# Seven block products instead of eight in the down projection of the last four feed-forward units

## The chip, the cores and the metric

The kernel runs on one NeuronCore of a Trainium2 chip. The metric is the device time of one execution in microseconds. The engines that matter here are PE (matrix multiplication, with PEld as its weight loads), DVE and ACT (element-wise work, and the copies out of the matmul accumulators in PSUM), POOL (a few small instructions) and SP (which issues most DMAs). Each engine works through its own queue in order and waits at an instruction until what it needs is there.

## The reference

Two layers, each a gated long convolution over the sequence followed by a feed-forward block (SwiGLU), on 2048 rows of 512 columns; the second layer uses the same weights as the first.

```python
def _A_ref(q, k, v, shift_k, ssm_k, ssm_D):
    ...                                  # k_shift: 4-tap convolution of k along the sequence
    kv = k_shift * v
    ...                                  # y: causal convolution of kv with ssm_k over 2048 rows, by FFT
    y = y + kv * ssm_D[None, None, :]
    return q * y

def _B_ref(x, w_gate, w_up, w_down):
    g = _silu(x @ w_gate)
    u = x @ w_up
    return (g * u) @ w_down              # (2048 x 512) -> 1792 -> 512

x = A_q
x = x + _A_ref(_layernorm(x), A_k, A_v, A_shift_k, A_ssm_k, A_ssm_D)
x = x + _B_ref(_layernorm(x), B_w_gate, B_w_up, B_w_down)
x = x + _A_ref(_layernorm(x), A_k, A_v, A_shift_k, A_ssm_k, A_ssm_D)
x = x + _B_ref(_layernorm(x), B_w_gate, B_w_up, B_w_down)
```

The outputs are bf16.

## The kernel before

The sequence is cut into four blocks `c` of 512 rows, and each block into two halves `h` of 256 rows. A half is two row tiles of 128 rows. Convolution and feed-forward of the blocks are interleaved: while PE multiplies for the feed-forward of one block, DVE and ACT prepare the spectra of the next. A feed-forward *unit* is `(layer, c, h)`; there are 16, and the last four, of block 3, are (0,3,0), (0,3,1), (1,3,0) and (1,3,1). By then no convolution is left, only the rows' normalisation, the gating of the convolution's result and the feed-forward itself.

Before a unit stands its prologue (`prologue`, with `ln_stats`, `normalise`): statistics of the rows of `x` (L846, L847, L849 on DVE), their inverse standard deviation `rstd` on POOL (L851), the normalised rows `n` times the convolution's rows `Yk` (L923), added to `x` (L924), again statistics and `rstd`, normalised rows `z` (L901), and a transposing DMA from SP (L930) into `zT`. So the rows that one unit of layer 0 leaves in `x` are needed by the prologue of the unit of layer 1 with the same `c` and `h`.

A unit (`ffn`) has 14 feature tiles of 128, in groups of 4, 4, 4 and 2 (`GROUPS`). For each pair of tiles 8 matmuls of 256 columns make the gate and 8 the up projection (L348) into a PSUM bank each (`pf`, four banks). ACT applies silu to the gate into `sg` (L1005) and copies the up projection to `ht` (L1009). DVE multiplies the two for a whole group (L1012): `ht` then holds the hidden tile, transposed, bf16. The down projection (L1025) takes the hidden tile as the loaded weights and a row tile of `w_down`, 512 columns, as the moving operand: for each feature tile and each of the two row tiles one matmul, accumulated over 14 feature tiles in a bank `pd` for each row tile. ACT copies both banks to `dn` (L1065), DVE adds them to `x` (L1068), and in layer 1 SP sends the rows to the output (L1076).

The last unit (1,3,1) differs at its end: its second row tile is split into two halves of columns with a bank each, the right half gets `x` by a matmul with the identity (L980), ACT copies it out (L1039), DVE adds the left half to `x` (L1041) and the first row tile (L1032), and the two halves leave by SP and ACT (L1045).

The order on each engine isn't left to a scheduler: the program records operations with their readers and writers, and the table `ORDER` of one number for each operation, found offline by a search, gives the order in which all are issued. Buffers come from rings (`s8` with 10 large slots, `ht` with 5, the PSUM rings `pf`, `pc`, `pd` with 4, 2 and 2 banks); a slot is taken again when its last reader is done. While PE would wait at the start, `issue` puts in warm-up matmuls (`wm`, L1297).

Of the kernel before, what the change touches and what calls it, by code (L numbers as in the profile page):

```python
# [9 lines left out]
P = 128  # L10
# [17 lines left out]
GROUPS = (4, 4, 4, 2)  # L28
TINY = 0.2
# [22 lines left out]
    4, 74, 3, 1, 2, 22, 16, 12, 14, 0, 13, 15, 40, 7, 6, 5, 8, 9, 17, 11, 18, 19, 10, 20, 21, 25, 41, 42, 56, 57, 34, 35, 33, 36, 31, 32, 29, 30, 51,  # L52
    53, 52, 70, 38, 39, 45, 48, 23, 24, 26, 64, 60, 46, 44, 61, 55, 43, 66, 76, 73, 47, 37, 82, 27, 28, 62, 63, 58, 68, 54, 65, 49, 50, 59, 69, 79,
    168, 199, 216, 243, 275, 75, 93, 94, 95, 96, 80, 89, 90, 91, 92, 77, 78, 81, 84, 85, 97, 98, 99, 100, 101, 104, 103, 105, 110, 125, 134, 147, 148,
    149, 166, 178, 71, 102, 111, 116, 117, 119, 120, 121, 67, 87, 83, 88, 72, 86, 106, 107, 108, 109, 112, 113, 114, 130, 131, 132, 144, 145, 146,
    139, 140, 141, 135, 136, 137, 126, 127, 128, 118, 122, 124, 123, 115, 133, 152, 155, 161, 156, 170, 175, 138, 129, 153, 154, 142, 143, 150, 151,
    158, 160, 157, 163, 159, 164, 171, 179, 162, 165, 197, 198, 188, 211, 212, 213, 176, 167, 177, 182, 219, 227, 169, 173, 172, 174, 180, 181, 183,
    184, 189, 190, 228, 229, 208, 209, 191, 231, 210, 185, 195, 186, 192, 193, 187, 196, 194, 202, 203, 220, 224, 225, 226, 221, 222, 238, 223, 230,
    232, 242, 233, 246, 247, 268, 263, 269, 267, 270, 271, 273, 274, 272, 281, 283, 284, 304, 316, 317, 311, 312, 248, 255, 257, 256, 259, 258, 261,
    260, 214, 215, 234, 205, 206, 207, 200, 201, 204, 217, 218, 236, 325, 326, 235, 249, 321, 324, 295, 296, 308, 309, 290, 292, 299, 300, 237, 285,  # L60
    327, 329, 354, 355, 368, 367, 276, 302, 375, 613, 303, 262, 305, 319, 320, 353, 369, 373, 374, 418, 432, 413, 433, 434, 460, 459, 465, 502, 473,
    495, 494, 514, 522, 524, 556, 557, 523, 542, 536, 500, 581, 650, 626, 651, 264, 265, 244, 245, 239, 240, 250, 251, 266, 323, 322, 252, 253, 241,
    254, 278, 288, 286, 287, 289, 336, 331, 291, 294, 293, 306, 297, 298, 279, 280, 307, 337, 332, 301, 310, 313, 314, 315, 338, 333, 339, 334, 342,
    352, 366, 350, 351, 360, 361, 346, 357, 378, 422, 399, 386, 387, 402, 403, 385, 388, 364, 365, 407, 423, 430, 406, 411, 404, 405, 384, 395, 396,
    397, 412, 424, 431, 340, 341, 344, 345, 371, 437, 439, 438, 440, 441, 347, 343, 348, 356, 349, 358, 359, 370, 376, 377, 381, 382, 383, 389, 391,
    390, 393, 394, 409, 410, 419, 420, 414, 415, 451, 452, 444, 445, 453, 461, 463, 462, 464, 466, 467, 471, 470, 472, 476, 477, 501, 545, 496, 544,
    447, 450, 448, 449, 488, 489, 487, 492, 493, 509, 506, 468, 469, 491, 498, 479, 481, 456, 457, 499, 510, 534, 482, 511, 454, 486, 504, 512, 474,
    475, 517, 537, 535, 518, 519, 505, 515, 541, 584, 563, 585, 596, 624, 667, 625, 427, 421, 428, 458, 478, 484, 485, 528, 530, 532, 533, 551, 553,
    538, 540, 554, 564, 573, 574, 565, 567, 400, 503, 277, 282, 531, 560, 599, 561, 619, 620, 622, 623, 621, 648, 649, 661, 662, 723, 689, 724, 318,
    330, 335, 328, 362, 380, 392, 379, 363, 398, 372, 401, 436, 480, 483, 490, 416, 417, 408, 426, 442, 443, 425, 429, 521, 548, 598, 597, 552, 601,  # L70
    603, 618, 529, 507, 513, 516, 497, 446, 435, 520, 569, 526, 571, 508, 455, 525, 527, 539, 555, 572, 578, 617, 612, 580, 579, 652, 641, 727, 728,
    717, 718, 683, 688, 676, 677, 665, 684, 643, 644, 642, 656, 731, 732, 733, 734, 778, 765, 769, 781, 674, 543, 750, 1069, 668, 657, 670, 671, 697,
    678, 698, 699, 796, 790, 805, 806, 807, 834, 835, 846, 880, 847, 891, 895, 888, 881, 892, 894, 889, 890, 896, 910, 902, 905, 925, 900, 926, 938,
    943, 949, 996, 995, 999, 1000, 1023, 1006, 1024, 1067, 582, 583, 591, 592, 568, 586, 558, 559, 600, 610, 629, 590, 595, 549, 550, 588, 589, 593,
    594, 602, 615, 630, 604, 605, 562, 587, 608, 609, 546, 570, 614, 616, 636, 575, 576, 547, 566, 577, 627, 639, 628, 640, 653, 654, 655, 645, 659,
    606, 607, 631, 638, 646, 658, 660, 696, 702, 672, 673, 675, 681, 685, 686, 637, 647, 687, 706, 703, 611, 692, 690, 691, 664, 666, 633, 635, 693,
    707, 704, 680, 694, 679, 682, 695, 710, 705, 711, 708, 712, 760, 766, 763, 764, 744, 745, 743, 757, 767, 797, 791, 779, 780, 729, 730, 738, 739,
    771, 772, 782, 799, 801, 770, 783, 725, 726, 792, 794, 755, 756, 795, 800, 808, 788, 802, 786, 803, 804, 814, 812, 815, 813, 816, 716, 719, 714,
    720, 721, 722, 741, 740, 746, 747, 748, 751, 752, 761, 762, 768, 773, 784, 820, 785, 798, 818, 819, 817, 823, 824, 825, 842, 850, 843, 853, 855,
    862, 864, 856, 863, 865, 866, 882, 886, 908, 883, 884, 830, 831, 839, 840, 827, 828, 845, 848, 849, 877, 874, 857, 858, 832, 833, 821, 829, 838,  # L80
    844, 867, 878, 876, 861, 871, 854, 870, 869, 873, 851, 852, 887, 903, 893, 868, 872, 875, 885, 901, 904, 942, 921, 961, 963, 1053, 964, 735, 709,
    736, 737, 809, 810, 811, 911, 906, 912, 913, 914, 918, 915, 922, 923, 924, 937, 947, 948, 945, 946, 700, 701, 713, 715, 742, 753, 754, 776, 822,
    930, 931, 973, 967, 974, 984, 989, 990, 992, 1004, 1068, 1003, 1008, 634, 663, 632, 669, 774, 759, 749, 758, 859, 860, 775, 777, 933, 934, 787,
    789, 932, 952, 793, 837, 826, 836, 841, 879, 957, 958, 959, 960, 962, 981, 1074, 1018, 897, 899, 927, 907, 975, 898, 928, 991, 988, 1001, 1037,
    985, 1022, 987, 983, 1007, 1030, 1038, 1039, 1099, 1097, 1110, 1098, 1101, 1136, 1121, 1122, 1116, 1117, 1193, 1194, 1111, 1112, 1167, 1168, 1185,
    1186, 1166, 1170, 1189, 1190, 1197, 1196, 1219, 1218, 1217, 1213, 1086, 1077, 1078, 1079, 1137, 1149, 1083, 1151, 1152, 1220, 1239, 1252, 1253,
    1265, 1272, 1273, 1274, 1275, 1276, 1279, 1291, 1282, 1283, 1280, 1281, 1284, 1285, 1292, 1305, 1322, 1329, 941, 953, 916, 935, 950, 951, 909,
    920, 954, 978, 994, 968, 982, 969, 970, 976, 977, 917, 936, 986, 1011, 1009, 971, 972, 979, 980, 965, 966, 955, 956, 998, 1012, 1016, 939, 940,
    919, 929, 944, 1014, 1028, 1015, 1029, 1031, 1033, 1032, 1025, 1026, 1027, 1034, 997, 1035, 1002, 1005, 1036, 1057, 1056, 1010, 1013, 1050, 1051,
    1044, 1045, 1040, 1041, 1052, 1059, 1062, 1054, 1055, 1046, 1049, 1047, 1048, 1042, 1043, 1058, 1060, 1063, 1019, 1020, 993, 1017, 1021, 1061,  # L90
    1064, 1066, 1065, 1080, 1070, 1088, 1073, 1089, 1071, 1075, 1072, 1076, 1105, 1153, 1131, 1118, 1133, 1113, 1114, 1108, 1109, 1128, 1132, 1142,
    1154, 1155, 1139, 1141, 1134, 1135, 1100, 1115, 1093, 1119, 1145, 1156, 1159, 1147, 1148, 1091, 1092, 1150, 1157, 1160, 1158, 1161, 1162, 1081,
    1082, 1084, 1085, 1090, 1095, 1103, 1102, 1104, 1106, 1120, 1124, 1107, 1123, 1125, 1126, 1144, 1163, 1138, 1140, 1174, 1176, 1173, 1175, 1178,
    1179, 1181, 1180, 1182, 1183, 1203, 1198, 1206, 1211, 1207, 1212, 1221, 1222, 1223, 1224, 1225, 1187, 1188, 1171, 1172, 1184, 1195, 1199, 1201,
    1202, 1216, 1234, 1204, 1205, 1208, 1226, 1214, 1215, 1227, 1228, 1235, 1236, 1241, 1230, 1231, 1164, 1165, 1200, 1237, 1209, 1210, 1240, 1259,
    1242, 1229, 1243, 1191, 1192, 1244, 1266, 1245, 1286, 1264, 1302, 1512, 1342, 1094, 1087, 1129, 1146, 1130, 1169, 1238, 1246, 1249, 1247, 1250,
    1293, 1294, 1295, 1298, 1296, 1299, 1300, 1308, 1309, 1328, 1310, 1311, 1143, 1177, 1096, 1127, 1232, 1233, 1330, 1314, 1331, 1332, 1343, 1344,
# [178 lines left out]
def kernel(  # L276
# [639 lines left out]
    def prologue(layer, c, h, on_pe=False):  # L916
# [47 lines left out]
        return done, [stats]  # L964


    LAST_UNIT = (1, NB - 1, HP - 1)

    def ffn(unit):
        layer, c, h = unit  # L970
# [360 lines left out]
```

## Time and profile before

| what | value |
|---|---|
| time, median of 3 runs | 344.43 us (343.92 to 344.95) |
| profiled execution: span from first to last instruction | 342.6 us (no own time beside the span is given) |
| PE busy | 337.9 us, 99% |
| DVE busy | 283.0 us, 83% |
| ACT busy | 252.3 us, 74% |
| gate and up projections (L348, pf) | 1792 matmuls, 57.1% of the chain that ended last |
| down projection (L1025, pd) | 462 matmuls, 28.2% of the chain |

The span is the time between the core's first and last instruction; the measured time also has what lies around it. Busy time of PE counts matmuls that overlap each other, so it says that PE had work, not how fast it went; the pace is read from long stretches of one kind in the chain. A chain is followed back from the last instruction, at each step to what released it. In a group of instructions the columns are: line, engine, operation, output and inputs, shapes, count, then busy time in us and the mean of one in ns, then the engine's idle time just before them and what ended it.

### The profile page before, as it was taken

How to read it: one execution, taken by the hardware profiler on the slowest of the kernel's cores; microseconds unless marked ns; L12 is line 12 of the kernel's file. 1: busy time of each engine (PE TensorE's matmuls, PEld its weight loads, DVE VectorE, ACT ScalarE, POOL GpSimd, SP SyncE). 2: the span in 40 equal slices, each digit the busy share in tenths (PEclk: the TensorE clock that was granted, in tenths of full speed). 3: DMA queues.
4: the chain of work that ended last, by engine and by line, in shares of the span. 5: the costliest groups of instructions: out<-in, count | busy, mean ns of one | idle time of the engine just before them, and what ended most of it. 6: DMA issues, size and time to landing. Idle time of an engine off the chain costs nothing.

```text
span 342.6 us, 6609 instructions
## 1 busy us (share of the span) xinstructions
PE 337.9 (99%) x2622; PEld 248.3 (72%) x2622; DVE 283.0 (83%) x482; ACT 252.3 (74%) x504; POOL 39.7 (12%) x46
## 2 busy tenths in 40 slices
PE   8999999999999999999999999999999999999996
PEld 7647867768686767768587767768675877777783
DVE  7999999999999999999999999989996524635122
ACT  6899999999984768868999955959474655446351
POOL 3000110103010101221010100100601000000000
PEclk9999999999999999999999999999999999999999
DMA  7999015130116056010101047000102010101001
GB/s 281 323 311 337 5 30 96 31 94 0 34 31 124 33 122 124 3 29 2 33 17 34 15 141 106 12 20 1 34 0 47 16 49 0 42 6 25 10 15 46
DMA packets 42088, 22.95 MB, mean 67 GB/s; under 512 B 33861, under 2 KB 39882, under 8 KB 42058
## 3 DMA queue, kind: packets, MB, share of 16 engines
q1 hardware_dynamic: 41904, 22.47, 26.2%
q8 instruction: 20, 0.33, 0.4%
q14 instruction: 10, 0.08, 0.1%
q10 hardware_dynamic: 154, 0.07, 0.1%
HBM read 12.33 MB, written 2.10 MB: 42 GB/s over the span
## 4 chain that ended last, share of the span: by engine, by line
PE 98%; ACT 1%; DVE 0%; issue 0%
PE pf L348 57%; PE pd L1025 28%; PE ps L348 8%; PE ps L495 2%; PE ps L834 1%; PE wm L1297 1%; ACT hs L524 1%; ACT X L456 0%; PE pt L403 0%; PE ptz L957 0%; PE pt L514 0%; DVE hs L530 0%; ACT xc L1039 0%; ACT nmr L889 0%; PE pt L1162 0%
## 5 line engine op out<-in xcount | busy, mean ns | idle before, releaser
L348 PE MATMUL pf<-zT,wg_sb 128*128 128x256 bf16 x896 | 110.2, 273 | 0.0
L348 PE MATMUL pf<-zT,wu_sb 128*128 128x256 bf16 x896 | 109.9, 273 | 0.0
L1025 PE MATMUL pd<-wd_sb,ht 128*128 128x512 bf16 (+1 forms) x462 | 103.9, 373 | 0.0
L348 PEld LDWEIGHTS <-wg_sb 128*128 128x128 bf16 x896 | 87.7, 98 | 16.0
L348 PEld LDWEIGHTS <-wu_sb 128*128 128x128 bf16 x896 | 87.7, 98 | 15.9
L1005 ACT ACTIVATE sg<-pf 128x512 bf16<-128x512 f32 x112 | 66.5, 607 | 23.8 <-PE pf L348 19.1
L1025 PEld LDWEIGHTS <-ht 128*128 128x128 bf16 x462 | 45.1, 98 | 44.6 <-DVE ht L1012 1.2
L1009 ACT CAST ht<-pf 128x512 bf16<-128x512 f32 x112 | 64.5, 593 | 14.5 <-PE pf L348 14.2
L1012 DVE TENSOR_TENSOR ht<-ht,sg 128x1024 bf16<-128x1024 bf16 (+1 forms) x64 | 38.9, 618 | 23.0 <-ACT ht L1009 13.3
L851 POOL TENSOR_TENSOR rstd<-ve,nhalf 128x2 f32<-128x2 f32 x24 | 27.7, 1155 | 210.3 <-DVE ve L849 210.3
L1065 ACT CAST dn<-pd 128x512 bf16<-128x512 f32 x30 | 17.1, 591 | 33.8 <-PE pd L1025 23.7
L846 DVE BATCH_NORM_STATS2 bnst<-xc 128x6 f32<-128x512 bf16 x48 | 31.6, 684 | 0.7
L690 DVE TENSOR_TENSOR t<-X,G 128x2048 bf16<-128x2048 bf16 x18 | 22.0, 1220 | 0.1
L694 DVE TENSOR_TENSOR t<-X,G 128x2048 bf16<-128x2048 bf16 x18 | 21.9, 1217 | 0.0
L1068 DVE TENSOR_TENSOR xc<-xc,dn 128x1024 bf16<-128x1024 bf16 x15 | 10.2, 682 | 12.1 <-ACT dn L1065 12.1
L456 ACT ACTIVATE X<-ps 128x512 bf16<-128x512 f32 x32 | 19.2, 608 | 0.7 <-PE ps L495 0.5
L877 POOL TENSOR_TENSOR rstd<-ve,nhalf 128x2 f32<-128x2 f32 x8 | 8.6, 1080 | 60.1 <-ACT ve L875 60.1
L923 DVE TENSOR_TENSOR n<-n,Yk 128x1024 bf16<-128x1024 bf16 x15 | 10.4, 690 | 6.1 <-ACT Yk L728 5.2
L704 DVE TENSOR_TENSOR Z<-Z,t 128x2048 bf16<-128x2048 bf16 x12 | 14.7, 1223 | 0.3
L702 DVE TENSOR_TENSOR t<-t,t 128x2048 bf16<-128x2048 bf16 x12 | 14.7, 1223 | 0.3
L456 ACT ACTIVATE H<-ps 128x512 bf16<-128x512 f32 x24 | 13.9, 619 | 0.0
L348 PE MATMUL ps<-hs,fwd 128*128 128x512 bf16 x40 | 12.8, 379 | 0.5 <-ACT hs L524 0.3
(105 smaller groups left out, 323.4 us busy)
## 6 DMA issues: line engine op xcount, KB each, us to landing
hn<-in_A_ssm_k_dram SPq DMA_DIRECT2D x4, 512.0 KB, 5.9
vt<-in_A_v_dram SPq DMA_DIRECT2D x4, 512.0 KB, 6.1
xc<-in_A_q_dram SPq DMA_DIRECT2D x4, 512.0 KB, 6.9
out_dram<-xc SPq DMA_DIRECT2D x15, 128.0 KB, 1.8
wg_sb<-in_B_w_gate_dram SPq DMA_DIRECT2D x1, 1792.0 KB
wu_sb<-in_B_w_up_dram SPq DMA_DIRECT2D x1, 1792.0 KB, 8.2
wd_sb<-in_B_w_down_dram SPq DMA_DIRECT2D x1, 1280.0 KB, 13.1
kn<-in_A_k_dram SPq DMA_DIRECT2D x1, 512.0 KB, 4.7
```

Source lines behind the costliest of these rows:

```text
L348: nc.tensor.matmul(o, lhsT=lhsT, rhs=rhs, start=(n == 0), stop=(n == len(terms) - 1))
L456: add("ACT", act(D), lambda: nc.scalar.activation(out=view(), in_=ps.t[:], func=ACT.Copy, scale=scale), r=[ps], w=[(buf, keys)], conv=conv)
L690: dve(n * D, lambda t1=t1, part=part: nc.vector.tensor_mul(out=t1.t[:], in0=x.t[:, sl, 0, :], in1=g.t[:, sl, part, :]), [(x, key(slots, (0 ...
L694: dve(n * D, lambda t2=t2, part=part: nc.vector.tensor_mul(out=t2.t[:], in0=x.t[:, sl, 1, :], in1=g.t[:, sl, 1 - part, :]), [(x, key(slots ...
L702: dve(n * D, lambda t1=t1, t2=t2, comb=comb: nc.vector.tensor_tensor(out=t1.t[:], in0=t1.t[:], in1=t2.t[:], op=comb), [t2], [t1], conv=conv)
L846: add("DVE", 0.6, lambda st=st, i=i: nc.vector.bn_stats(out=st.t[:], in_=xs[c].t[:, i, :]), r=[(xs[c], (i,))], w=[st])
L851: add("POOL", pw, lambda: nc.gpsimd.tensor_tensor(out=rstd.t[:], in0=ve.t[:], in1=nhalf.t[:].to_broadcast((P, n)), op=ALU.pow), r=[ve, nha ...
L1005: add("ACT", act(D), lambda ps=ps, o=o, sg=sg: nc.scalar.activation(out=sg.t[:, o:o + 2, :], in_=ps.t[:], func=ACT.Silu), r=[ps], w=[(sg, ...
L1009: add("ACT", act(D), lambda ps=ps, o=o, ht=ht: nc.scalar.copy(out=ht.t[:, o:o + 2, :], in_=ps.t[:]), r=[ps], w=[(ht, (o // 2,))], due=(uni ...
L1012: dve(n * W, lambda sg=sg, ht=ht: nc.vector.tensor_mul(out=ht.t[:], in0=ht.t[:], in1=sg.t[:]), [sg], [ht], due=(unit, k / pairs, 0.0, "h"))
L1025: nc.tensor.matmul((pds[o] if not cs.start else pds[HP]).t[:, cs], lhsT=ht.t[:, q, o * P:(o + 1) * P], rhs=wt["d"].t[:, ft, cs], start=(ft ...
L1065: add("ACT", act(D), lambda o=o: nc.scalar.copy(out=dn.t[:, o, :], in_=pds[o].t[:]), r=[pds[o]], w=[(dn, (o,))], due=(unit, 1.0, 3.0, "h"))
```

## The change

For block 3 the down projection of a pair of feature tiles and the two row tiles, a product of 2 x 2 blocks (row tile x feature tile times feature tile x half of the columns), is computed by Strassen's scheme in its seven-product form: seven matmuls of 256 columns where there were four of 512 (eight blocks). `STRASSEN` says for how many groups of each unit: all four for (0,3,0), (0,3,1) and (1,3,0), the first two for (1,3,1). 25 pairs of feature tiles are meant.

`weight_sums` makes, once, sums and differences of blocks of `w_down` for all pairs, in three slots of `s8`. `seven` makes for each group five sums and differences of hidden tiles (`cb`) on DVE and issues the products into four PSUM banks `ps7` (two of `pd`, two of `pc`), two products side by side in three of them. `add_seven` copies the four banks to SBUF on ACT (`mt`) and adds them into `x` with five DVE instructions; it takes the place of the copies to `dn` and the one addition. In the last unit the products come first, the last two groups go as before, and the identity matmul (`first_half`) stands behind `add_seven`, as it reads the `x` that this leaves. The table `ORDER` is a new one for the whole program.

```diff
+STRASSEN = {(0, 3, 0): 4, (0, 3, 1): 4, (1, 3, 0): 4, (1, 3, 1): 2}
...
 ORDER = [
...
+    C = D // 2
+    ws = {}
+
+    def weight_sums():
...
+        ev = lambda sl: wd.t[:, 0::2, sl]
+        od = lambda sl: wd.t[:, 1::2, sl]
+        lo, hi = slice(0, C), slice(C, D)
+        a = ws["14"] = new("s8", "wsa", [P, 2, NF // 2, C], parts=2)
+        b = ws["3"] = new("s8", "wsb", [P, NF // 2, C])
+        c = ws["67"] = new("s8", "wsc", [P, NF, C])
+        for out, keys, x0, x1, op in (
+                (lambda: a.t[:, 0], [(a, (0,))], lambda: ev(lo), lambda: od(hi), ALU.add),
+                (lambda: b.t[:], [b], lambda: ev(hi), lambda: od(hi), ALU.subtract),
+                (lambda: a.t[:, 1], [(a, (1,))], lambda: od(lo), lambda: ev(lo), ALU.subtract)):
+            dve(NF // 2 * C, lambda out=out, x0=x0, x1=x1, op=op: nc.vector.tensor_tensor(out=out(), in0=x0(), in1=x1(), op=op),
+                [wd], keys)
...
+    def seven(unit, banks, ht, fts, first, last):
+
+        m = len(fts) // 2
+        f0 = fts[0] // 2
+        cb = new("s8", "cb", [P, 5, m, P], parts=3)
+        e, q, r, o = banks
...
+        dve(2 * m * P, lambda: nc.vector.tensor_add(
+            out=strided(cb.t[:], 0, [[P, m], [m * P, 2], [1, P]]), in0=strided(ht.t[:], 0, [[2 * W, m], [P, 2], [1, P]]),
+            in1=strided(ht.t[:], W, [[2 * W, m], [P, 2], [1, P]])), [ht], [(cb, (0,))], **kw)
...
+        for bank, rd, terms in (
+                (e, [ht, ws["14"], ws["3"]], (
+                    (0, lambda i: ht.t[:, 2 * i + 1, P:2 * P], lambda i: ws["14"].t[:, 1, f0 + i]),
+                    (1, lambda i: ht.t[:, 2 * i, 0:P], lambda i: ws["3"].t[:, f0 + i]))),
+                (q, [(cb, (0,)), wd], (
+                    (0, lambda i: cb.t[:, 0, i], lambda i: wd.t[:, 2 * (f0 + i) + 1, C:D]),
+                    (1, lambda i: cb.t[:, 1, i], lambda i: wd.t[:, 2 * (f0 + i), 0:C]))),
+                (r, [(cb, (1,)), ws["67"]], (
+                    (0, lambda i: cb.t[:, 3, i], lambda i: ws["67"].t[:, 2 * (f0 + i) + 1]),
+                    (1, lambda i: cb.t[:, 2, i], lambda i: ws["67"].t[:, 2 * (f0 + i)]))),
+                (o, [(cb, (2,)), ws["14"]], (
+                    (0, lambda i: cb.t[:, 4, i], lambda i: ws["14"].t[:, 0, f0 + i]),))):
+            def go(bank=bank, terms=terms):
+                for half_, lhsT, rhs in terms:
+                    for i in range(m):
+                        nc.tensor.matmul(bank.t[:, half_ * C:(half_ + 1) * C], lhsT=lhsT(i), rhs=rhs(i),
...
+    def add_seven(unit, banks):
...
+        for n, bank in enumerate(banks):
+            k = C if n == 3 else D
+            add("ACT", act(k), lambda n=n, bank=bank, k=k: nc.scalar.copy(out=mt.t[:, n, 0:k], in_=bank.t[:, 0:k]), r=[bank], w=[(mt, (n,))],
...
+        dve(2 * D, lambda: nc.vector.tensor_add(out=x.t[:, span(rows), :], in0=x.t[:, span(rows), :],
+                                                in1=mt.t[:, 0:1, :].to_broadcast((P, 2, D))), [(mt, (0,))], [(x, rows)], **kw)
+        dve(D, lambda: nc.vector.tensor_add(out=strided(x.t[:], at + C, [[1, D]]), in0=strided(x.t[:], at + C, [[1, D]]), in1=mt.t[:, 1]),
+            [(mt, (1,))], [(x, rows)], **kw)
+        dve(D, lambda: nc.vector.tensor_sub(out=two(2), in0=two(2), in1=two(1)), [(mt, (1,))], [(mt, (2,))], **kw)
+        dve(D, lambda: nc.vector.tensor_add(out=two(2), in0=two(2), in1=mt.t[:, 3:4, 0:C].to_broadcast((P, 2, C))), [(mt, (3,))],
+            [(mt, (2,))], **kw)
+        dve(D, lambda: nc.vector.tensor_add(out=ends(), in0=ends(), in1=two(2)), [(mt, (2,))], [(x, rows)], **kw)
...
             dve(n * W, lambda sg=sg, ht=ht: nc.vector.tensor_mul(out=ht.t[:], in0=ht.t[:], in1=sg.t[:]), [sg], [ht],
                 due=(unit, k / pairs, 0.0, "h"))
+            if gi < sevens:
+                seven(unit, banks, ht, fts, gi == 0, gi == sevens - 1)
+                if gi == sevens - 1:
+                    add_seven(unit, banks)
+                    if unit == LAST_UNIT:
+                        first_half()
+                continue
...
     for c in range(NB):
+        if (0, c, 0) == min(STRASSEN):
+            weight_sums()
         run((0, c, 0))
```

## The prediction

> **What bounds the kernel now.** I read the page's busy times and slices first, then the chain of waits in order of time, then the windows of the last stage, then the groups by form and the timeline of POOL. All durations below are from that one profiled execution. Its span is 342.6 us; no time of its own is given beside the span, so I put the sum against the median of the runs, 344.43, and carry the 1.8 us that lie around the span unchanged (the three runs lie between 343.92 and 344.95).
>
> ```profile
> PE 337.9 (99%) x2622; PEld 248.3 (72%) x2622; DVE 283.0 (83%) x482; ACT 252.3 (74%) x504; POOL 39.7 (12%) x46
> ...
> DVE  7999999999999999999999999989996524635122
> ACT  6899999999984768868999955959474655446351
> ...
> PEclk9999999999999999999999999999999999999999
> ```
>
> PE is busy throughout, at full granted clock. DVE is full for about three quarters of the span and half idle in the last quarter. The chain says where PE's time counts one to one:
>
> ```profile
> 22.47 0.91 ACT hs L524
> 23.38 0.04 issue
> ...
> 33.37 7.87 PE pf L348 x72
> ...
> 285.14 11.35 PE pf L348 x104
> 296.50 6.04 PE pd L1025 x28
> 302.54 6.99 PE pf L348 x64
> ...
> 333.15 6.09 PE pd L1025 x42
> 339.24 0.02 issue
> 339.26 0.37 ACT xc L1039
> ```
>
> From 33.37 to 339.24 the chain is PE alone. It gives PE's pace: 11.35/104 = 109.1 ns for a matmul of 256 columns, 6.04/28 = 215.7 ns for one of 512. The last stretch agrees: 14 of 512 and 28 of 256 columns (also with ht loaded as weights) make 6.08, shown 6.09. Only before 33 us does PE wait for others, and after 339.24 come one copy and the last output DMA.
>
> ```profile
> 200.00:225.00 25.00, 25.00 (x181) 17.42 (x179) 24.66 (x40) 14.86 (x32) 1.75 (x2) 1.00 0.47 95
> ...
> 280.00:290.00 10.00, 10.00 (x70) 6.74 (x69) 3.23 (x9) 4.09 (x8) 0.69 (x1) 1.00 0.00 0
> 290.00:300.00 10.00, 10.00 (x77) 7.35 (x75) 6.37 (x14) 4.87 (x9) 0.69 (x1) 1.00 0.17 41
> ```
>
> The columns are PE, PEld, DVE, ACT, POOL. Until 250 us DVE has no room (24.66 of 25); between 260 and 330 the seven windows of 10 us leave DVE 41.6 us and ACT 35.4 us idle. The four units of block 3, which the change touches, run there.
>
> ```profile
> L1012 DVE TENSOR_TENSOR ht<-ht,sg 128x1024 bf16<-128x1024 bf16 x48 | 32.8, 685 | 19.3 <-ACT ht L1009 13.3 <-ACT sg L1005 6.0
> ...
> L1065 ACT CAST dn<-pd 128x512 bf16<-128x512 f32 x30 | 17.1, 591 | 33.8 <-PE pd L1025 23.7 <-DVE xc L1068 6.0 <-issue 4.1
> ...
> L561 DVE TENSOR_TENSOR vt<-ps,vt 128x512 bf16<-128x512 f32 x4 | 2.7, 692 | 0.4 <-PE ps L348 0.4
> ...
> L1012 DVE TENSOR_TENSOR ht<-ht,sg 128x512 bf16<-128x512 bf16 x16 | 6.7, 418 | 3.6 <-ACT sg L1005 3.6
> ...
> L1041 DVE TENSOR_TENSOR xc<-xc,pd 128x256 bf16<-128x256 bf16 x1 | 0.4, 420 | 0.4 <-PE pd L1025 0.4
> ```
>
> **The change part by part.**
>
> *PE.* By the instruction lists 92 matmuls of 512 columns and 16 of 256 go, 175 of 256 come: -92 x 0.2157 - 16 x 0.1091 + 175 x 0.1091 = -2.5 us. (One pair of feature tiles cost 4 x 215.7 = 863 ns and costs 7 x 109.1 = 764; 25 pairs.) Every matmul has its own weight load of 98 ns, which the x104 stretch hides under 109 ns; so it should here, as long as the weights are there in time.
>
> *Start.* The new order issues 0.32 us less PE work ahead of the first gate matmul (two warm-up matmuls and one of 512 columns, the latter moved behind it). That part waits for ACT and DVE, so leaving work out gains nothing. DVE's list up to the normalised rows z that the first unit needs has the same instructions in another order. I take the first gate matmul at the same 33.2 us; then what follows it shrinks by 2.5 - 0.2 = 2.3 us. Bounds: PE stood still for 0.5 us in the first 24 us besides the 0.76 at the start, and filled 0.7 more with warm-up matmuls at 22.4, so a better order could win 1.2 there; a worse one could lose the length of one late ACT step, 0.9 (hs in the chain).
>
> *Weight sums.* Five DVE instructions of 1792 elements; between 685 ns (1024) and 1220 ns (2048, L690) that is 1.09 each, 5.4 us. They stand on DVE behind the row update of (0,3,1)'s prologue, at about 266 to 275 us, where DVE begins to be idle; the first product that needs them is due on PE at about 278.5. Cover: 3 us.
>
> *Sums of ht (seven).* 22 instructions of 512 elements, 17 of 256, 3 of 128, with runs of 128. No row shows such runs. Lower end: as for long runs, 418 ns for 512, and on the line through 685 and 418, 285 and 220 for the smaller: 14.7 us. Upper end: one element a cycle as in L561 and L1041, 692 and 420 ns: 23 us. I take the lower, since the inputs are bf16 in SBUF with step 1 as in L1012, where L561 and L1041 read f32 from PSUM. The Trainium skill (VectorE: DVE Perf Modes, "What auto-detection actually checks") has the two-a-cycle mode hang on 16-bit type and step of one, without a word on run length, so by it the lower end and the sum below stand; no run here shows it yet.
>
> *Result (add_seven).* Per unit DVE has 1 x 0.685 + 4 x 0.418 = 2.36 where it had 0.685 (the last unit had none): +7.4 us. ACT has 3 x 0.591 + 0.372 instead of 2 x 0.591: +5.1 us over four units. Sums: DVE +27.5 into 41.6 idle, ACT +5.1 into 35.4.
>
> *Do they meet PE's dates?* PE runs its queue in order, so one late sum holds all gate matmuls behind it. I laid the new lists out by hand from the rows, with PE at its pace:
> - End of (0,3,0): ACT copies the last needed hidden tile at 278.5; nine DVE instructions follow, 0.69 + 0.42 + 0.42 + 0.29 + 0.42 + 0.15 + 0.29 + 0.42 + 0.29, with the last sums at 281.7 and 282.0, wanted at 282.0 and 282.9. Slack 0.3.
> - (0,3,0) to (1,3,0): the o bank ends at 284.3; ACT copy, two adds, statistics, rstd, n, two row passes, statistics, rstd, z, transpose DMA (2.4) with the new sums between end at about 299.6; the first gate matmul of (1,3,0) wants zT at 301.0. Slack 1.4. Before, z was done at 295.8 for a start at 302.5.
> - (0,3,1) to (1,3,1): 314.7 against 317.6, slack 3.
> - The last unit: its seven products now come after nearly all gate matmuls, and the identity matmul that feeds the row into its bank waits for the whole result chain. PE has 0.76 (seven delayed products of (1,3,0)) + 1.29 to do; ACT copy 0.37, two dependent DVE adds 0.84 and hand-overs need 1.6 to 1.8. Slack 0.3. If that cover went, each 0.1 us late is 0.1 us of the end.
> - SP: both rows of (1,3,0) leave only at about 335.7, ahead of the last unit's rows in SP's queue; at 0.33 to 0.58 for an issue (L1076, median 0.43) the fourth begins between 336.7 and 337.4, where its data allow 337.0. Between 0 and +0.4; I take +0.2, in the middle, as other slacks of 0.3 stand beside it.
>
> Sum: -2.3 + 0.2 = -2.1; 344.43 - 2.1 = **342.3**.
>
> **The rivals.**
>
> *A: rstd on POOL stretches (no change).* POOL's rstd lies twice on each path from a unit's result to the next zT.
>
> ```profile
> 240.54 4.20 POOL L851 TENSOR_TENSOR rstd<-ve,nhalf 128x2 f32<-128x2 f32 x1 [1.58 <-DVE ve L849]
> ...
> 288.86 0.69 POOL L851 TENSOR_TENSOR rstd<-ve,nhalf 128x2 f32<-128x2 f32 x1 [17.11 <-DVE ve L849]
> ```
>
> The same instruction took 0.69 us where DVE was waiting and up to 4.20 where DVE was full; all five from 271 us on took 0.69. Now DVE has work queued behind ve. My chain has 1.2 to 1.4 for each; at 1.53 (common in the full stage) nothing is lost, at 4.20 once, the path is 2.9 late against 1.4: +1.5, 343.8. For it: DVE's new load; against: the new list puts n or z, which wait for rstd, two or three instructions behind ve, so DVE must fall idle soon. The Trainium skill (SBUF — State Buffer, "Who interferes with whom") calls the port pair of DVE and GpSimd an exclusive lock, held for the whole instruction. By that rule, the trace agrees (4.20 against 0.69), and the sum stands only while DVE pauses for rstd. Chance 0.13.
>
> *B: DVE is too late at the units' ends (slower).* If the sums run at one element a cycle, those of 512 grow by 0.27, of 256 by 0.135. At the end of (0,3,0) that makes 1.15 against a slack of 0.3: 0.8 lost; in (0,3,1) the last group's sums are 2.1 later against 0.4: 1.7; (1,3,0) waits for ACT anyway: 0; in the last unit 1.5 against 0.3: 1.2. Together +3.7: 346.0. It decides against the gain from about 0.15 us more per sum. For it: no row shows short runs, and the slacks are thin; against: the types. Chance 0.12.
>
> *C: the new order costs PE in the first 250 us (no change).* DVE was full there, so a prologue that comes later starves PE. DVE's work ahead of each z and PE's ahead of each unit's start stand within about 1 us of before at the tight places (6.4 and 6.3 us between them where before had 6.6 to 7.8). With 0.9 at the start and as much in the middle: 344.1. Chance 0.08.
>
> *D: the product count saves nothing*, as weight loads of 98 ns leave only 11 ns. The x104 stretch speaks against it; at 123 ns (110.2/896, the page's busy time over count, which counts overlaps) a pair would cost 861: 344.6. Chance 0.02.
>
> **How the numbers follow.** Forecast 0.65, its own range 341.5 to 343.3 (0.6 gained at the start and SP at 0; 0.2 more by SP and 0.8 by the thin slacks). A 0.13, B 0.12, C 0.08, D 0.02. A measurement tells 0.3% (1.03 us) from no change: faster is below 343.4. That is the forecast and a third of A and C, where less is lost: 0.72. The rest of A and C, and D: 0.16. B: 0.12. The range 341.5 to 344.5 leaves out B and the forecast's own outer 0.08.
>
> **What would show it.** Right: 175 matmuls ps7 in stretches at 109 ns; PE's work after the first gate matmul 2.3 us shorter; DVE some 27 us busier, in the last quarter; sums of ht at about 418 ns. Wrong: the sums at 690 (B); a gap of PE before (1,3,0)'s first gate matmul, released by the transpose DMA (A); PE waiting for a DVE sum at a unit's end, or for x at the identity matmul; the first gate matmul later than 33.7 (C); the last output issue more than 0.5 behind the last copy (SP).

## The result and the profile after

The changed kernel takes 341.91 us (median; 341.58 to 342.03) against 344.43 us before: 0.9922 of the time, with a 95% interval of 0.9909 to 0.9936. On another chip (the run after_again below) the ratio was 0.9915 [0.9902, 0.9929]. It is faster by 2.5 us by the medians of this measurement, 2.7 by the ratio. One of its five executions took 390.47 us at a granted clock of 0.851; it is left out of the range and the ratio, as are one of e2 (1267.34) and one of e8 (352.2) below. The profiled execution took 342.03 us with a span of 340.3, where the span before was 342.6: 2.3 us less.

The page of the changed kernel, busy times and slices:

```profile
PE 334.0 (98%) x2657; PEld 255.4 (75%) x2687; DVE 304.7 (90%) x546; ACT 257.9 (76%) x514; POOL 38.3 (11%) x46
...
DVE  8899999999999998999999999999998787968255
...
PEclk9999999999999999999999999999999999999999
```

The last quarter of DVE, ten slices that read 6524635122 before, now reads 8787968255: the new work went where DVE had been idle. One thing has to be known before PE is read here: there are 2687 weight loads but only 2657 matmuls. Each matmul has one load, so 30 matmul records are missing. Each leaves a gap that looks like a wait of PE, and the chain of waits leaves PE there and wanders over DVE, ACT and POOL. So for this kernel I read PE's stalls from the weight loads, which are complete: the start of each load is set against the sum of the paces (215.7 and 109.1 ns) of the matmuls ahead of it. Where the difference grows, PE stood.

From 277 us on the chain is PE alone again:

```profile
279.16 4.80 PE ps L1031 x44
...
284.95 11.36 PE pf L353 x104
296.31 5.35 PE ps L1031 x49
301.65 7.86 PE pf L353 x72
...
335.92 1.32 PE pd L1126 x12
```

The products (L1031) run at 4.80/44 and 5.35/49 = 109.1 and 109.2 ns, the gate matmuls at 11.36/104 = 109.2. No unit's end shows a wait for a sum. The small jumps in between, such as 301.65 against 301.49 where the first gate matmul of (1,3,0) starts, are places of missing records.

The one stall that the weight loads show after the start is at 56.76 us, in the timeline of PE and in the waits of PE's weight loads:

```profile
56.76 0.39 PE L353 MATMUL ps<-hs,fwd 128*128 128x512 bf16 x1 [0.42 <-DMA hs<-hr]
```

```profile
PEld L353 <- DMA hs<-hr: 0.7, 1, 0.7
```

PE stood 0.60 us behind a transposing DMA of block 2's rows, in a part of the kernel that the seven products do not touch. Before, the same matmul started at 58.02 with no wait.

The sums and the additions, in the groups by form:

```profile
L1009 DVE TENSOR_TENSOR cb<-ht 128x512 bf16<-128x512 bf16 x11 | 4.6, 420 | 0.2
L1006 DVE TENSOR_TENSOR cb<-ht 128x512 bf16<-128x512 bf16 x11 | 4.5, 420 | 0.2
L1012 DVE TENSOR_TENSOR cb<-ht 128x256 bf16<-128x256 bf16 x11 | 3.0, 284 | 0.1
...
L989 DVE TENSOR_TENSOR wsa<-wd_sb 128x1792 bf16<-128x1792 bf16 x2 | 2.2, 1082 | 0.0
...
L1055 DVE TENSOR_TENSOR xc<-xc,mt 128x512 bf16<-128x512 bf16 x4 | 1.7, 425 | 0.1
...
L1012 DVE TENSOR_TENSOR cb<-ht 128x128 bf16<-128x128 bf16 x3 | 0.7, 219 | 0.0
```

Where the 2.3 us of span went, cut at the first gate matmul and at PE's last matmul:

| stretch | before | after | change |
|---|---|---|---|
| up to the first gate matmul | 33.22 | 32.90 | -0.32 |
| from there to the end of PE's last matmul | 306.02 | 304.34 | -1.68 |
| behind PE's last matmul | 3.36 | 3.06 | -0.30 |

The middle row is 2.48 less work by the counts and paces, plus 0.22 for the matmul of 512 columns that moved behind the first gate matmul, plus the stall of 0.60: -1.66.

### The profile page after: what moved, and what is told of

The parts are those of the page before. It is cut to its first block, busy times and chain, and to the rows that moved or that the text cites. A ratio compares the mean times of both kernels' runs of the same rounds, so it can differ in the third digit from the quotient of the medians.

```text
span 340.3 us, 6793 instructions
## 1 busy us (share of the span) xinstructions
PE 334.0 (98%) x2657; PEld 255.4 (75%) x2687; DVE 304.7 (90%) x546; ACT 257.9 (76%) x514; POOL 38.3 (11%) x46
## 4 chain that ended last, share of the span: by engine, by line
PE 70%; DVE 12%; ACT 11%; issue 3%; POOL 2%; DMA 1%; POOLq 0%; ACTq 0%
PE pf L353 41%; PE pd L1126 16%; PE ps L1031 6%; PE ps L353 5%; ACT X L461 2%; DVE bnst L851 1%; DVE t L707 1%; DVE Z L709 1%; DVE m L582 1%; DMA hs<-hr 1%; ACT H L461 1%; ACT ht L1103 1%; PE wm L1402 1%; DVE ht L1106 1%; PE ps L500 1%
## 5 line engine op out<-in xcount | busy, mean ns | idle before, releaser
L1103 ACT CAST ht<-pf 128x512 bf16<-128x512 f32 x112 | 65.2, 591 | 29.1 <-PE pf L353 26.8
L1099 ACT ACTIVATE sg<-pf 128x512 bf16<-128x512 f32 x112 | 65.8, 605 | 23.4 <-PE pf L353 21.5
L1126 PE MATMUL pd<-wd_sb,ht 128*128 128x512 bf16 (+1 forms) x331 | 80.2, 375 | 1.1
L1126 PEld LDWEIGHTS <-ht 128*128 128x128 bf16 x354 | 34.6, 98 | 32.2
L856 POOL TENSOR_TENSOR rstd<-ve,nhalf 128x2 f32<-128x2 f32 x24 | 26.5, 1103 | 210.8 <-DVE ve L854 210.8
L1168 ACT CAST dn<-pd 128x512 bf16<-128x512 f32 x24 | 13.4, 592 | 9.7 <-PE pd L1126 9.7
L1043 ACT CAST mt<-ps 128x512 bf16<-128x512 f32 (+1 forms) x16 | 8.3, 536 | 9.4 <-PE ps L1031 9.3
L882 POOL TENSOR_TENSOR rstd<-ve,nhalf 128x2 f32<-128x2 f32 x8 | 8.4, 1051 | 59.9 <-ACT ve L880 59.9
L1031 PEld LDWEIGHTS <-cb 128*128 128x128 bf16 x125 | 12.2, 98 | 1.4
```

The source lines that it names most:

```text
L856: add("POOL", pw, lambda: nc.gpsimd.tensor_tensor(out=rstd.t[:], in0=ve.t[:], in1=nhalf.t[:].to_broadcast((P, n)), op=ALU.pow), r=[ve, nha ...
L1031: nc.tensor.matmul(bank.t[:, half_ * C:(half_ + 1) * C], lhsT=lhsT(i), rhs=rhs(i), start=(first and i == 0 and half_ == 0), stop=(last and ...
L1099: add("ACT", act(D), lambda ps=ps, o=o, sg=sg: nc.scalar.activation(out=sg.t[:, o:o + 2, :], in_=ps.t[:], func=ACT.Silu), r=[ps], w=[(sg, ...
L1103: add("ACT", act(D), lambda ps=ps, o=o, ht=ht: nc.scalar.copy(out=ht.t[:, o:o + 2, :], in_=ps.t[:]), r=[ps], w=[(ht, (o // 2,))], due=(uni ...
L1126: nc.tensor.matmul((pds[o] if not cs.start else pds[HP]).t[:, cs], lhsT=ht.t[:, q, o * P:(o + 1) * P], rhs=wt["d"].t[:, ft, cs], start=(ft ...
```

## The experiments

The theory: the gain is the 2.5 us of columns on PE and nothing else; all that the change adds to DVE and ACT is hidden; the new order has one misplaced wait. The rivals: the gain came from the new order of the whole program; the sums cost something that does not show; the covers are wide (or thin) in another way than the prediction laid them out.

**The seven products alone, and the new order alone.** The operations ahead of the first gate matmul of (0,3,0) are the same 1327 in both kernels, but for a few, so the two parts of the change can be taken apart there. In e6 these have the old order and the seven products follow; in e5 they have the new order and eight block products follow in their old order.

```diff
 # e6_old_head_seven: the changed kernel
-ORDER = [...]   # as searched
+ORDER = [...]   # first 1327 operations as in the kernel before, the rest as in the changed kernel
 # e5_new_head_eight: the kernel before
-ORDER = [...]   # as in the kernel before
+ORDER = [...]   # first 1327 operations as in the changed kernel, the rest as in the kernel before
```

> The changed kernel with the first 1327 of its operations in the order of the kernel before, and the seven products and the rest as in the changed kernel. It is the seven products by themselves. Theory: 2.5 us less than before on PE and 0.2 less behind PE's last matmul, no stall at 57 us, first gate matmul at 33.2 as before: 341.7 to 342.0. Rival (the order search is where the gain came from): 344.

> The kernel before (eight block products everywhere), with the first 1327 of its operations, those ahead of the first gate matmul of unit (0,3,0), in the order that the changed kernel gives them; the rest in the order of before. It is the new order of the first 260 us by itself. Theory (the columns saved on PE are the gain; the new order by itself gives 0.3 at the start and loses 0.2 to 0.6 behind the DMA at 57 us): 344.3 to 344.9, the same as before. Rival (the order search is where the gain came from): 342 to 343.

e6 took 341.86 us, 0.9921 [0.9908, 0.9935] of before: the whole gain. e5 took 344.49, 1.000 [0.9991, 1.0009]: none of it. The chain of e6 has the same stretches as the changed kernel, and no stall at 57 us:

```profile
284.62 11.36 PE pf L361 x104
295.98 5.35 PE ps L1039 x49
```

In the same place the chain of e5 has its down projection in matmuls of 512 columns (5.99 us are 27.8 of them at 215.7 ns, one more than the record counts):

```profile
285.56 11.35 PE pf L356 x104
296.97 5.99 PE pd L1033 x27
```

The rival of the order search is out for these operations, the first 260 us; behind them the order is new wherever the products are, and there the next run tells the columns from the order. The two parts add up, by the medians: -2.6 and 0.1 against -2.5 and -2.8 for both together on two chips.

**The eighth product put back as time.** The product that has a bank half to itself is issued twice, the second time into the half that nothing reads.

```diff
                         nc.tensor.matmul(bank.t[:, half_ * C:(half_ + 1) * C], lhsT=lhsT(i), rhs=rhs(i),
...
+                        if len(terms) == 1:
+                            nc.tensor.matmul(bank.t[:, C:D], lhsT=lhsT(i), rhs=rhs(i), start=False, stop=(last and i == m - 1))
```

> The changed kernel with the seventh product of every pair issued a second time into the unused half of its bank: 25 matmuls of 256 columns more, nothing else. Theory (the gain is the count of columns on PE): 25 x 109.1 ns = 2.7 us more, 344.6, that is the time of the kernel before. Rival (the gain came from the new order, or PE has room in the last stage): clearly less than 2.7 more, 342 to 343.5.

It took 344.45 us, 0.9997 [0.9988, 1.0006] of before. The busy times of the page have 25 matmuls more:

```profile
PE 337.9 (99%) x2712; PEld 257.0 (75%) x2712; DVE 305.1 (89%) x546; ACT 257.8 (75%) x514; POOL 38.2 (11%) x46
```

Twenty-five matmuls of 256 columns, in the same order, take the whole gain away again: 2.5 us by the medians for 25 x 109.1 ns = 2.7. The price of a column on PE is paid in full in the last stage, as far as the intervals tell.

**The sums taken away.** All five products that read `cb` load slices of `w_up` instead, and each of the 42 sums is cut to 8 elements.

```diff
-        dve(2 * m * P, lambda: nc.vector.tensor_add(
...
+        for key, at in ((0, 0), (1, 2), (2, 4)):
+            dve(8, lambda at=at: nc.vector.tensor_add(out=cb.t[:, at, 0, 0:8], in0=ht.t[:, 0, 0:8], in1=ht.t[:, 1, 0:8]), [ht], [(cb, (key,))], **kw)
...
-                    (0, lambda i: cb.t[:, 0, i], lambda i: wd.t[:, 2 * (f0 + i) + 1, C:D]),
+                    (0, lambda i: wt["u"].t[:, i, 0:P], lambda i: wd.t[:, 2 * (f0 + i) + 1, C:D]),
...
```

> The changed kernel without the sums of hidden tiles: the 42 DVE instructions that make cb are cut to 8 elements each, and the five products of each pair that read cb load slices of w_up instead, so the down projection of block 3 is not computed. DVE has some 12 us less to do, and no product waits for a sum. Theory (the sums are hidden to the last): the same 341.9, within 0.2. Rival (they hold PE up at the units' ends or in the last unit): 0.5 to 1 us less.

It took 341.75 us, 0.9921 [0.9908, 0.9934]: the same as the changed kernel. Its page has 7.6 us less DVE (304.7 to 297.1) and nothing of that on the path:

```profile
PE 335.2 (99%) x2687; PEld 254.7 (75%) x2687; DVE 297.1 (87%) x546; ACT 257.6 (76%) x514; POOL 39.2 (12%) x46
```

The products still wait for the short sums, 0.16 us each, as the program still records that they read `cb`; the run takes away the length of the sums, not the waits. So that length is hidden to the last. How much more would have been hidden is the next question.

**The sums made longer.** A part of each sum is done a second time.

```diff
+        def sums(n, op, out, in0, in1, key):
+            def go():
+                nc.vector.tensor_tensor(out=out(n), in0=in0(n), in1=in1(n), op=op)
+                nc.vector.tensor_tensor(out=out(1), in0=in0(1), in1=in1(1), op=op)
+            dve(n * m * P, go, [ht], [(cb, (key,))], **kw)
...
```

> The changed kernel with a part of every sum of hidden tiles done twice (256 elements more for groups of four tiles, 128 for groups of two, 42 instructions more): each sum grows by 0.28 or 0.22 us, some 11.4 us on DVE in all, a little more than the forecast's case of one element a cycle (+8). Theory (slacks of 0.3 to 0.4 as the prediction laid them out): 1.1 lost at the end of (0,3,0), 1 to 2.5 at the end of (0,3,1), 1 to 1.8 at the end of (1,3,1): 345 to 347. Rival (DVE's pauses and the late places of the products take it up): less than 1 us, under 343.

It took 346.71 us, 1.0063 [1.0051, 1.0075]: slower than the kernel before, by 1.4% more than the changed kernel. The timeline of PE, only the three pieces that begin after the longest waits, from 262 us on:

```profile
282.55 0.39 PE L1032 MATMUL ps<-wd_sb,cb 128*128 128x256 bf16 x2 [0.54 <-DVE cb L1009]
...
301.73 0.83 PE L1032 MATMUL ps<-wd_sb,cb 128*128 128x256 bf16 x6 [1.21 <-DVE cb L1009]
...
336.50 1.68 PE L1032 MATMUL ps<-wsa,cb 128*128 128x256 bf16 x11 [0.41 <-DVE cb L1009]
...
```

Each idle time in the brackets is short of the loss, as a matmul's end is modelled; by the weight loads PE lost 0.95 us at the end of (0,3,0), 1.59 at the end of (0,3,1), 0.51 at the end of (1,3,0) and 1.77 in the last unit: 4.8 us. The second and the fourth are in the ranges expected, the first is 0.15 below the 1.1 expected, and the third was expected at nothing. The first of these places gives the slack of the changed kernel: the sum that its products wait for ended 2.47 us behind the start of its group's multiplication in the changed kernel and 3.97 us in e4 (282.49 against 278.52), 1.50 later; 0.72 was lost at that matmul, so 0.78 had been free. DVE's busy time grew by 10.6 us (304.7 to 315.3).

**The misplaced wait.** The first matmul on block 2's rows changes place with the group of up-projection matmuls behind it.

```diff
-ORDER[561], ORDER[372] = 353, 354   # ps<-hs, then pf<-zT,wu_sb
+ORDER[561], ORDER[372] = 354, 353
```

> The changed kernel with one swap in its order: the first matmul on the transposed rows of block 2 (op 561, ps<-hs, where PE stood 0.60 us behind the transposing DMA at 56.8) goes behind the next up-projection group (op 372, 0.87 us of PE work). Theory (PE's queue is the bound everywhere after 33 us, so a stall of PE counts in full): 0.6 us less, 341.3. Rival (the copies of ACT or the four pf banks behind that place are as late, so the stall only moves): 0.2 us less or nothing, 341.7 to 341.9.

It took 341.40 us, 0.9911 [0.9898, 0.9924], and no weight load waits for the DMA any more. That is 0.4 to 0.5 below the changed kernel, less than the intervals can tell apart, so it ran once more beside the changed kernel itself:

> The changed kernel as it is, on the chip of its neighbours here: 341.9 by its first measurement. The PE stand behind the transposing DMA at 57 us was 0.60, 0.51, 0.23 and 0.32 in four profiles with that order: between 0.2 and 0.6 here.

> The changed kernel with the first matmul on the transposed rows of block 2 behind the next up-projection group, once more, beside the changed kernel on the same chip. Theory: less than the changed kernel by what PE stood at 57 us there, 0.2 to 0.6: 341.3 to 341.7. Rival: the same as the changed kernel within 0.1.

There the two took 341.62 (0.9915) and 341.38 (0.9909). The stall in that profile of the changed kernel was 0.25 us; in seven profiles with this order and seven products it was 0.60, 0.51, 0.32, 0.31, 0.25, 0.23 and 0.17, as the DMA landed earlier or later against PE. In the timeline of e1_again PE goes through without a gap:

```profile
55.13 1.91 PE L361 MATMUL pf<-zT,wu_sb 128*128 128x256 bf16 x16
56.88 0.38 PE L361 MATMUL ps<-hs,fwd 128*128 128x512 bf16 x1
```

The trace shows the stall gone; that the time is shorter by it, 0.2 to 0.5 us, fits both measurements and is not told from nothing by either. It has the lowest median here, by a margin that the measurement does not settle.

**Work behind `ve`.** For the rival that `rstd` on POOL stretches, DVE additions whose results are unused are put right behind the second `ve` of (1,3,0): three of 2048 elements, or eleven of 512.

```diff
             st = ln_stats_act(c, rows) if ST2(layer, c, h) else ln_stats(c, rows)
+            if (layer, c, h) == (1, 3, 0):
+                dm, wd = new("t4", "dm", [P, 4, D]), wt["d"]
+                def filler():
+                    for _ in range(3):      # e8: range(11), with 0:1, 0:1 and 4:5
+                        nc.vector.tensor_add(out=dm.t[:, 0:4], in0=wd.t[:, 0:4], in1=wd.t[:, 4:8])
+                add("DVE", 3.6, filler, r=[wd], w=[dm])
```

> The changed kernel with three DVE additions of 2048 elements (some 3.6 us, results unused) right behind the second ve of (1,3,0), so that DVE has no pause while POOL makes rstd. Theory of rival A as the prediction told it (POOL gets on only where DVE pauses): rstd takes 3.6 us or more, where it took 0.73. Other reading (POOL gets on between two DVE instructions, so the length of one DVE instruction matters): 1.2 to 2. The sums of (0,3,1) behind it on DVE come 3.6 us late; with the slack of 0.4 that the prediction gave them the time is about 3 us longer, 345, and with the 2 us that the rows of z leave less.

> The same with eleven DVE additions of 512 elements in place of the three of 2048: the same DVE time in short instructions. Theory of rival A as told: rstd 3.6 us or more here too. Other reading (between two DVE instructions): 0.7 to 1.0. Time as in its neighbour, about 345.

The timeline of POOL, first in e7, then in e8:

```profile
296.76 1.53 POOL L864 TENSOR_TENSOR rstd<-ve,nhalf 128x2 f32<-128x2 f32 x1 [5.38 <-DVE ve L862]
```

```profile
294.11 0.73 POOL L864 TENSOR_TENSOR rstd<-ve,nhalf 128x2 f32<-128x2 f32 x1 [5.38 <-DVE ve L862]
```

DVE worked at the additions for 3.73 us behind `ve` in e7 and for 5.01 in e8 (eleven at 0.456, where I had reckoned with 3.6 in all). But it was not without a pause there: the additions all write the same output, and 0.03 to 0.04 us lie between two of them (three of 1.22 us are 3.67 of the 3.73). In both runs `rstd` ended 0.55 us behind the first such pause, after 1.53 us beside the long additions and 0.73 beside the short ones. So e7 and e8 do not test what they were made for, whether POOL needs a pause of DVE.

The other rows of the twelve profiles do, 372 instructions `rstd` from 24 us on. None of them passed a pause of DVE, however short (some are of 0.03 us): it ended at the latest 0.55 us behind it. Between two DVE instructions without a pause 186 got on, again 0.55 us behind the end of the first, but 24 such places were passed. All seven that took more than 1.7 us (1.90 to 6.18) had passed at least one and ended behind a pause. One of the seven lies in e7, in layer 0, far ahead of the additions; the first line is the same instruction in the changed kernel, the others are e7:

```profile
37.90 1.55 POOL L882 TENSOR_TENSOR rstd<-ve,nhalf 128x2 f32<-128x2 f32 x1 [6.95 <-ACT ve L880]
```

```profile
37.74 3.83 POOL L890 TENSOR_TENSOR rstd<-ve,nhalf 128x2 f32<-128x2 f32 x1 [6.95 <-ACT ve L888]
...
43.31 1.03 PE L361 MATMUL pf<-zT,wg_sb 128*128 128x256 bf16 x8 [2.11 <-ACT ht L1117]
```

DVE did the same work beside both, two instructions `G` and one `t` of 2048 elements without a pause. In the changed kernel `rstd` got on behind the first `G`. In e7 it passed the ends of both and ended 0.55 us behind the end of `t`, where DVE paused; ACT, which needs `rstd`, was late with its copy of the up projection, and PE stood 2.27 us by the weight loads. So the reading of rival A as told is too strict, since POOL mostly gets on without a pause, but its mechanism stands: in these profiles POOL was sure to get on only at a pause, and in e7 PE paid for the places that it passed.

The times were 345.8 (343.97 to 347.72) and 346.8 us (345.02 to 347.98), about as expected, but with a wide spread, of which more below; the profiled execution of e7 is its slowest, 347.72, and holds the 2.27 us. In e8 PE lost 3.45 us at the first product that waited for a sum, in e7 2.17; the sum came 4.9 and 3.6 us later there than in the changed kernel (295.46), PE's own shift taken off, so in the middle of (0,3,1) the slack is 1.5 us. No gate matmul of the last stage waited for `zT` in either.

## Why the prediction was right

The forecast was 342.3 us and the likeliest case came: the range held both medians, 341.91 and 341.62. Step by step:

- *PE, -2.5.* Right, and shown by e2 and e6: by counts and paces 2.48, the products at 109.2 ns with their weight loads of 98 ns hidden. Rival D is out.
- *Start.* The prediction left the first gate matmul at 33.2 and so gave 0.2 back. It was at 32.90, and in nine of ten profiles with the new first part between 32.50 and 32.92 (33.21 in e5); the two with the old one had 33.22 and 33.39. So this term was too high by 0.3 us in the profile. Whether the work left out ahead of it shortened that part is not shown: e5 leaves out the same and begins at 33.21, and why the others came earlier was not tried.
- *Weight sums.* 1.06 to 1.08 us each, forecast 1.09, between 265 and 275 us as told; hidden.
- *Sums of `ht`.* 420, 284 and 219 ns, where the lower end was 418, 285 and 220: runs of 128 elements cost nothing here. The rule of the Trainium skill (VectorE: DVE Perf Modes, "What auto-detection actually checks"), type and step alone, agrees with these rows.
- *`add_seven`.* DVE 2.38 us a unit, forecast 2.36; ACT 589 and 374 ns, forecast 591 and 372. The durations of all DVE instructions add up to 27.0 us more, forecast 27.5; its busy time grew by 21.7 only (283.0 to 304.7), since instructions that follow each other without a pause overlap in the records and are counted once.
- *Covers.* At the end of (0,3,0) the sum that was due first ended at 281.42 for products at 282.28; the slack forecast at 0.3 was 0.8 by e4. Towards (1,3,0) the prediction had zT at 299.6 and wanted at 301.0; the second row of z was done at 296.78, but SP was at the first row's DMA until 297.37 and issued the second at 297.47, so with its 2.4 it landed at 299.9, for a gate matmul at 301.49. In the last unit `x` was ready at 335.19 for the identity matmul at 335.64: 0.45 less a hand-over, forecast 0.3. All held.
- *SP at the end, +0.2.* Wrong: the fourth issue began at 337.50 with its data done at 337.47. It cost nothing. The part behind PE's last matmul was even 0.30 shorter, which no step had; 2.62 us lie behind the last ACT copy where 2.92 lay before (by the ends of the spans before rounding), and what of this belongs to the new end is open: e5, with the old end, had 2.75, e4, with the new one, 2.86.
- *Rival B.* The size was not there, but the mechanism was, and e4 shows it with its price: the forecast lost 3.7 us for 8 us of longer sums, the chip 4.8 for 11.4. Taken as a straight line from nothing, which is an estimate, the gain of 2.7 is used up when the sums are 6.4 us longer in all, 0.15 us a sum, as the prediction had it; with slacks of 0.8 and 1.5 us the loss sets in later than that line, so it may bear more, and no run lies between. The zero at (1,3,0) was wrong (0.51).
- *Rival A.* `rstd` took 0.93, 0.99, 0.73, 0.69 and 0.73 us in the last stage. That it was not realised there was forecast; the reason given, that DVE would pause, was wrong. DVE had no pause behind the second `ve` of (1,3,0), and `rstd` took 0.73: it got on between two short instructions. The rule of the Trainium skill (SBUF — State Buffer, "Who interferes with whom") speaks of a lock for the whole instruction, and read so, instruction by instruction, it agrees with 1.53 beside long instructions against 0.73 beside short ones. The 24 places that POOL passed it does not tell. Such passing made the 4.20 before (4.21 in e6, with the same order), and 6.17 and 6.18 at 241 us in after_again and e8, where the weight loads show no loss; why a place is passed in one execution and not in the next is open. So that A cost nothing in the changed kernel's profile is in part luck: in one of ten profiles with that order in the first 260 us, e7, it cost 2.27.
- *Rival C.* It came true in small, and where the prediction had seen no loss: the stall of 0.2 to 0.6 at 57 us. The prediction compared DVE's work ahead of each z and missed this transposing DMA. For the step "C costs nothing" the runs put +0.6 in the profile and +0.3 as the middle of seven.

So the mechanism was right, the columns saved on PE, but that the sum of -2.1 came so near to -2.3 was luck, as errors met: 0.3 at the start, 0.2 for SP and 0.3 behind PE's end were charged too much, 0.6 at 57 us too little.

## What to carry to other kernels

Where PE is dense, work taken from PE was worth its pace here, and it could be bought with work on engines that are idle in the same stage; e3 and e4 show that such a cover can be complete and still end less than a microsecond further on (0.8 us at the end of (0,3,0)). So lay out the dates at each unit's end, as a busy share of 70% in that stage says nothing of it. With a new order of the whole program, look for single new waits of PE far from the change, DMAs among them; and count the records first, since a missing matmul looks like a stall and its weight load tells the difference.

## What the runs showed of the hardware

In e7 PE's clock fell to half after PE had stood for 2.17 us, in the windows of 2 us from 298 to 308 (the columns are PE, PEld, DVE, ACT, POOL, then the granted clock):

```profile
298.00:300.00 2.00, 0.99 (x10) 0.64 (x7) 1.97 (x2) 0.60 (x1) 0.29 (x1) 1.00 0.00 0
300.00:302.00 2.00, 1.01 (x7) 0.77 (x7) 2.00 (x8) 0.00 (x0) 0.00 (x0) 0.82 0.00 0
302.00:304.00 2.00, 2.00 (x11) 1.45 (x10) 1.90 (x6) 0.00 (x0) 0.00 (x0) 0.50 0.33 66
304.00:306.00 2.00, 2.00 (x17) 1.66 (x16) 0.33 (x2) 0.52 (x1) 0.00 (x0) 0.83 0.51 131
306.00:308.00 2.00, 2.00 (x20) 1.79 (x19) 1.60 (x4) 1.57 (x4) 0.00 (x0) 1.00 0.00 0
```

For about 3.4 us the products came every 213 ns, and that cost 1.7 us on top of the wait. In e8 PE stood longer, 3.45 us, and the clock stayed at 1.00. The Trainium skill (TensorE: Matmul & The Clock Gate, "What's actually happening") has the clock at half after an idle window of some 3.4 us that runs free of the kernel; the length of the slow stretch agrees, but here a stand of 2.17 us was enough once and ones of 3.45 us and of 2.27 (e7 at 43.31 us, the clock at 1.00 in the windows from 42 to 46) were not. The granted clock that is on record for every execution fits: in e7 the two of 344.0 us had 0.999 and 1.000, the six of 345.3 to 347.7 all 0.995, and half a per cent of 344 us is the 1.7. In e8 five had 0.990 to 0.995 (346.4 to 348.0 us) and two 0.999, of 345.0 and 347.6, so the clock is not all of the spread. For this kernel it means that a long stall of PE can cost more than itself.
